# Weights converted with ScalarE's scaled high word and three VectorE operations, and new orders up to step 23

## The chip, the cores and the metric

The kernel runs on one core of a Trainium2 chip. The metric is the device time of one execution in microseconds (us), the median of several runs. The core has five engines that run side by side: TensorE (PE; matmuls, and PEld, its weight loads), VectorE (DVE), ScalarE (ACT), GpSimd (POOL) and SyncE (SP), which here issues the DMAs.

## The reference

A linear attention without a softmax, then two feed-forward layers, on 8 x 576 = 4608 tokens with 512 features. The weights come as float64 and q, k, v as float32.

```python
kv = np.einsum('bhsd,bhse->bhde', k, v)          # 8 x 8 heads, 576 tokens, 64 wide
out = np.einsum('bhsd,bhde->bhse', q, kv)
rms = np.sqrt(np.mean(out * out, axis=-1, keepdims=True) + 1e-06)
x = out / rms * g_norm                            # -> 4608 x 512

h = x @ w_in                                      # 512 x 2048
P = a[0] + a[1] * h + a[2] * h2 + a[3] * h3       # h2 = h*h, h3 = h2*h
Q = 1.0 + np.abs(b[0]) * np.abs(h) + np.abs(b[1]) * h2
x = (P / (Q + 1e-06)) @ w_out                     # 2048 x 512

h = (x @ w1) * (x @ w2) @ w3                      # 512 x 1024, 1024 x 1024
x = h @ w_out2                                    # 1024 x 512
```

## The kernel before

**Numbers.** Each matmul operand is split in a high and a low part (`hi`, `lo`, both in TensorE's reduced fp32 type), and a product is three matmuls. ScalarE casts the high part (L84), VectorE subtracts it for the low one (L85).

**Conversion of weights.** The chip gets a float64 weight as two 32-bit words, `hw` (sign, exponent and upper mantissa bits) and `lw`. `to_f32` (L144 to L165) builds the float32 from them; it is a generator that stops (`yield`) between its operations, so that a caller can put other work between them. `conv` runs it into a tile `ct` and queues the split of the weight, which is issued when two later conversions have gone ahead (`DEPTH`). There are 88 conversions: 32 of the first layer's `w_in` (`wa0` to `wa15`) and `w_out` (`wb0` to `wb15`), 32 of half the size for `w1` and `w2` in the background (`bg_conv`), and 24 for `w3` and `w_out2` (`cv_conv`).

**The start.** A string of letters (L458) sets the order in which work is issued until the first layer begins: `K` loads a tile of 128 tokens of k and v, `Q` one of q, `W` a weight, `C` converts one; `k` multiplies a tile into the batch's state (`kv`, copied into `kvbd`), `t` transposes q, `o` multiplies it with the state and squares the result, `r` and `n` make the norm and transpose it back, `x` writes the operand `xh`, `xl` of the first layer. A batch has 576 tokens, so its state needs four and a half tiles. All loads stand in SyncE's queue; k, v and q have two buffers each. Each engine works in the order in which its instructions were issued, and waits at the first whose inputs aren't there. Eleven of the 32 weights are converted here.

**The steps.** The first layer then runs in 192 steps `g` (12 blocks of 384 tokens by 16 slices of the 2048 columns). In step `g` TensorE does `l1(g)` (12 matmuls into `h`) and, three steps late, `l2(g - 3)` (12 matmuls into `acc`, which take `hi` and `lo`). Between them stands the function P/Q: `ew1(g)` on ScalarE (`a`, `z`, `n`), GpSimd (`s`, L543) and VectorE (L546, L548), `ewy(g)` on ScalarE, `ew2(g - 1)` on VectorE (L562, L564, L566) and `ew3(g - 2)`, which casts `hi` (L529) and subtracts `lo` (L531). The remaining 21 weights are converted in steps 0 to 22: a digit of `CONV` says how many in each step. The string `MIX[0]` says in which order the pieces of the generators are issued in these steps (`n` ew1, `l` ew3, `y` ewy, `s` ew2, `t` and `u` conversions); from step 23 on it is `MIX[1]`. Attention of later tiles is spread over the steps by a table (`at_step`).

After the first layer the second one runs in products of 256 columns (`c_slot`), then `w3` is multiplied with `w_out2`, and `d_slot` makes the output.

Of the kernel before, what the change touches and what calls it, by code (L numbers as in the profile page):

```python
# [12 lines left out]
AF = mybir.ActivationFunctionType  # L13
ALU = mybir.AluOpType
# [4 lines left out]
def linear_attention_two_moe_kernel(  # L19
# [24 lines left out]
    nc = tc.nc  # L44
# [35 lines left out]
    def f32(ap):  # L80
        return ap.bitcast(F32)
# [55 lines left out]
    def mix(order, **gens):  # L137

        for c in order:
            next(gens[c], None)  # L140
        for gen in gens.values():
            run(gen)

    def to_f32(raw, t, n=W):  # L144


        hw, lw = raw[:, :, 1], raw[:, :, 0]
        ti = t.bitcast(I32)
        nc.scalar.activation(out=ti, in_=f32(hw), func=AF.Copy, scale=0.47 * 2.0**15)
        nc.scalar.activation(out=t, in_=ti, func=AF.Sign)  # L150
        yield
        nc.vector.tensor_scalar(  # L152
            out=lw, in0=lw.bitcast(U32), scalar1=2.0**-29, scalar2=7.0, op0=ALU.mult, op1=ALU.min
        )
        yield
        nc.vector.scalar_tensor_tensor(
            out=lw, in0=hw, scalar=3, in1=lw, op0=ALU.logical_shift_left, op1=ALU.bitwise_or
        )
        yield
        nc.vector.tensor_scalar(  # L160
            out=lw, in0=lw, scalar1=0x7FFFFFFF, scalar2=0x40000000,
            op0=ALU.bitwise_and, op1=ALU.bitwise_xor,
        )
        yield
        nc.vector.tensor_tensor(out=t, in0=f32(lw), in1=t, op=ALU.mult)  # L165

    def f32_tile(n=W):
        return stp.tile([P, n], F32, tag="st", name="ct")
# [11 lines left out]
    def conv_flush():  # L180
        while pend:
            conv_on(0)

    def conv(raw, *stages):

        t = f32_tile(W)
        yield from to_f32(raw, t)
        pend.append((t, list(stages)))
        conv_on()
# [221 lines left out]
    with tc.manual_schedule():  # L411
# [23 lines left out]
        def w_next():  # L435
            kind, i = w_seq[n_cv[0]]
            n_cv[0] += 1
            return (conv_a if kind == "a" else conv_b)(i)
# [16 lines left out]
            "r": (n_rms, n_rsq), "n": (n_out, x_pe), "x": (x_out,),  # L455
        }
        whole = {"W": w_load, "C": w_conv, "F": conv_flush, "c": consts, "d": const_ops}
        for op in "KWCcKQkWKCWQWkCWtKQtkCKWFkdCkCoWWCQtoKoCrrnWCkWtKonKWrWWrCnxkKQWnQxxCxWW":  # L458
            if op in whole:
                whole[op]()  # L460
            else:
                i = count.get(op, 0)
                count[op] = i + 1
                for f in tile_ops[op]:
                    f(i)
# [93 lines left out]
        def ew2(g):  # L559
            e = st_[g]  # L560
            s, n, y = e["s"], e["n"], e["y"]
            nc.vector.scalar_tensor_tensor(out=s, in0=s, scalar=EPS_Q, in1=y, op0=ALU.add, op1=ALU.mult)  # L562
            yield
            nc.vector.scalar_tensor_tensor(out=n, in0=n, scalar=na[:, 0:1], in1=y, op0=ALU.add, op1=ALU.mult)  # L564
            yield
            nc.vector.scalar_tensor_tensor(out=n, in0=s, scalar=2.0, in1=n, op0=ALU.subtract, op1=ALU.mult)  # L566
# [12 lines left out]
        def do(g, place):  # L579
            for f, i in todo.get((g, place), ()):  # L580
                f(i)
# [17 lines left out]
        for i in range(T0, NTILE):  # L599
            j, t = divmod(i, TPB)  # L600
# [28 lines left out]
        def bg_conv(n):  # L629
            w = f32_tile(HW)  # L630
            yield from to_f32(bg_raw.pop(n), w, HW)
            nc.sync.dma_start(out=bg[n][2], in_=w)
# [221 lines left out]
        def cv_conv(n):  # L854
            w = f32_tile()
            run(to_f32(cv_raw.pop(n), w))
            nc.sync.dma_start(out=cv[n][1], in_=w)
# [185 lines left out]
                nc.scalar.copy(f["u"], f["b"])  # L1043
            e_load(n + 3)

        MIX = "nltutssnuyltntusutu", "nltysstnnltts"
        CONV = "11201102220020012111010"
        NG = NBA * MF
        LB = NG - MF
        prep = {}  # L1050
# [56 lines left out]
        for g in range(NG + SK):  # L1107
# [12 lines left out]
            if 0 <= g - 1 < NG:  # L1120
                gens["s"] = ew2(g - 1)
            if g < len(CONV):
                for x in "tuv"[:int(CONV[g])]:
                    gens[x] = w_next()
# [3 lines left out]
            if g - 2 in BG_AT:  # L1128
                gens["t"] = bg_conv(BG_AT.index(g - 2))
            mix("".join(x for x in MIX[g >= len(CONV)] if x in gens), **gens)  # L1130
            do(g, 2)
            do(g, 3)
            if g == len(CONV) - 1:
                conv_flush()
# [59 lines left out]
```

## Time and profile before

| | us |
|---|---|
| median of 3 runs | 1635.74 (1635.54 to 1637.78) |
| profiled execution, its own time | 1637.61 |
| its span | 1635.80 |
| TensorE busy (matmul) | 1550.0 (95%) |
| VectorE busy | 1337.7 (82%) |
| ScalarE busy | 1102.8 (67%) |
| GpSimd busy | 239.1 (15%) |

The span runs from the first to the last instruction of the profiled execution. Busy time is an average over stages with different limits: an engine that is busy for 82% of the span can be full in one stage and idle in the next. So the stages have to be looked at apart, and in each the question is which engine the others wait for. The granted clock is that of TensorE, as a share of full speed.

### The profile page before, as it was taken

The page shows a single profiled execution, that of the slowest core. Times are in us where ns is not written, and L with a number is a line of the kernel's source. Part 1 is how long each engine was busy: PE and PEld are TensorE (multiplying, and loading weights), DVE is VectorE, ACT ScalarE, POOL GpSimd, SP SyncE. Part 2 cuts the span into 40 slices and gives each one's busy share as a digit, 9 for nine tenths or more (in the row PEclk, how much of TensorE's full clock was granted, in tenths as well). Part 3 has the DMA queues.
Part 4 walks back from the last instruction along what each step waited for, and adds up shares of the span by engine and source line. Part 5 has one row for each costly group of instructions (what it writes and reads, how often), then busy time and mean ns, then how long its engine had stood idle before and what let it go on. Part 6 is the DMA issues. An engine that isn't in the chain of part 4 may idle for free.

```text
span 1635.8 us, 25683 instructions
## 1 busy us (share of the span) xinstructions
PE 1550.0 (95%) x9320; PEld 1506.2 (92%) x9320; DVE 1337.7 (82%) x2467; ACT 1102.8 (67%) x2197; POOL 239.1 (15%) x201
## 2 busy tenths in 40 slices
PE   4688899999999999999999998899999999999999
PEld 4687899999999999999999997899999998789999
DVE  5898987888989989999999889787677675578885
ACT  4787886787888888888878787554444443455554
POOL 0023322222222222222222221000000000000000
PEclk9798999999999999999999999999999999999999
DMA  9754234432111111111111011424534534334442
GB/s 243 188 148 126 58 79 103 104 81 59 52 30 52 32 51 43 52 49 39 40 42 54 6 46 36 139 91 152 186 104 158 169 112 139 117 125 155 156 158 88
DMA packets 202079, 157.92 MB, mean 97 GB/s; under 512 B 122848, under 2 KB 179936, under 8 KB 201952
## 3 DMA queue, kind: packets, MB, share of 16 engines
q1 hardware_dynamic: 201952, 156.28, 32.2%
q8 instruction: 73, 1.20, 0.3%
q14 instruction: 54, 0.44, 0.1%
HBM read 106.43 MB, written 49.81 MB: 96 GB/s over the span
## 4 chain that ended last, share of the span: by engine, by line
PE 67%; DVE 15%; ACT 3%; issue 2%; DMA 1%; POOL 0%; SPq 0%; DVEq 0%; ACTq 0%; POOLq 0%
PE acc L783 10%; PE h L90 6%; PE h L88 6%; PE h L89 6%; PE acc L496 5%; PE acc L991 5%; PE acc L493 5%; PE acc L494 5%; PE h L783 4%; PE kv L783 3%; PE at L783 3%; DVE n L564 3%; PE h L991 2%; DVE s L562 2%; PE kv L991 2%
## 5 line engine op out<-in xcount | busy, mean ns | idle before, releaser
L543 POOL TENSOR_TENSOR s<-z,a 128x384 f32<-128x384 f32 x192 | 237.5, 1237 | 774.5 <-ACT z L540 400.4
L564 DVE SCALAR_TENSOR_TENSOR n<-n,na,y 128x384 f32<-128x384 f32 x192 | 182.8, 952 | 0.0
L555 ACT ACTIVATE y<-s,epsq 128x384 f32<-128x384 f32 x192 | 118.2, 615 | 70.4 <-POOL s L543 70.2
L546 DVE TENSOR_TENSOR n<-n,h 128x384 f32<-128x384 f32 x192 | 104.8, 546 | 54.2 <-ACT n L541 54.1
L540 ACT ACTIVATE z<-a,ab 128x384 f32<-128x384 f32 x192 | 136.6, 711 | 6.4
L562 DVE SCALAR_TENSOR_TENSOR s<-s,y 128x384 f32<-128x384 f32 x192 | 134.3, 700 | 0.4
L539 ACT ACTIVATE a<-h 128x384 f32<-128x384 f32 x192 | 93.3, 486 | 54.3 <-PE h L90 52.0
L541 ACT ACTIVATE n<-h,na 128x384 f32<-128x384 f32 x192 | 126.2, 657 | 3.6 <-DVE lo L531 3.6
L548 DVE SCALAR_TENSOR_TENSOR n<-n,na,h 128x384 f32<-128x384 f32 x192 | 117.8, 614 | 6.0
L531 DVE TENSOR_TENSOR lo<-n,hi 128x384 fp32r<-128x384 f32 x192 | 106.2, 553 | 0.0
L566 DVE SCALAR_TENSOR_TENSOR n<-s,n 128x384 f32<-128x384 f32 x192 | 106.1, 553 | 0.0
L556 ACT ACTIVATE y<-y 128x384 f32<-128x384 f32 x192 | 101.2, 527 | 6.1
L529 ACT CAST hi<-n 128x384 fp32r<-128x384 f32 x192 | 96.6, 503 | 5.9 <-DVE n L566 5.8
L271 PE MATMUL kv<-vt,kt 128*128 128x128 f32 (+1 forms) x320 | 51.1, 310 | 14.8 <-DMA vt<-in_v_dram 13.9
L271 PEld LDWEIGHTS kv<-vt,kt 128*128 128x128 f32 (+1 forms) x320 | 47.7, 221 | 17.6 <-issue 12.2
L150 ACT ACTIVATE ct<-ct 128x512 f32<-128x512 int32 (+1 forms) x88 | 49.0, 556 | 2.8
L354 PE MATMUL at<-kvbd,qT 128*128 128x128 f32 (+1 forms) x216 | 28.7, 283 | 5.6 <-ACT qT L346 5.0
L354 PEld LDWEIGHTS at<-kvbd,qT 128*128 128x128 f32 (+1 forms) x216 | 26.3, 182 | 7.8 <-ACT qT L346 6.4
L825 ACT COPY p<-kv 128x384 f32<-128x384 f32 x24 | 11.5, 479 | 32.2 <-PE kv L783 20.7
L379 ACT ACTIVATE ny<-ms,epsn 128x8 f32<-128x8 f32 x36 | 11.1, 309 | 31.5 <-DVE ms L373 31.3
L840 ACT COPY u<-acc 128x384 f32<-128x384 f32 x24 | 11.5, 480 | 29.6 <-PE acc L783 29.5
L152 DVE TENSOR_SCALAR wb12r<-wb12r 128x512 int32<-128x512 uint32 x25 | 10.7, 427 | 24.8 <-DMA wb12r<-in_moe_w_dram 23.2
(1443 smaller groups left out, 5013.8 us busy)
## 6 DMA issues: line engine op xcount, KB each, us to landing
ed<-eo SPq DMA_DIRECT2D x48, 384.0 KB, 2.7
er<-ed SPq DMA_DIRECT2D x36, 512.0 KB, 3.8
x2d<-xev SPq DMA_DIRECT2D x48, 192.0 KB, 2.0
xr<-x2d SPq DMA_DIRECT2D x48, 192.0 KB, 4.0
out_dram<-o SPq DMA_DIRECT2D x36, 256.0 KB, 2.0
kt<-in_k_dram SPq DMA_DIRECT2D x32, 256.0 KB, 3.4
vt<-in_v_dram SPq DMA_DIRECT2D x32, 256.0 KB, 4.1
qt<-in_q_dram SPq DMA_DIRECT2D x32, 256.0 KB, 3.4
```

What stands on the lines that cost most here:

```text
L531: nc.vector.tensor_tensor(out=e["lo"], in0=e["n"], in1=f32(e["hi"]), op=ALU.subtract)
L540: nc.scalar.activation(out=z, in_=a, func=AF.Identity, scale=ab[:, 1:2], bias=ab[:, 0:1])
L541: nc.scalar.activation(out=n, in_=h, func=AF.Identity, scale=na[:, 3:4], bias=na[:, 2:3])
L543: nc.gpsimd.tensor_tensor(out=s, in0=z, in1=a, op=ALU.mult)
L546: nc.vector.tensor_tensor(out=n, in0=n, in1=h, op=ALU.mult)
L548: nc.vector.scalar_tensor_tensor(out=n, in0=n, scalar=na[:, 1:2], in1=h, op0=ALU.add, op1=ALU.mult)
L555: nc.scalar.activation(out=y, in_=e["s"], func=AF.Abs_reciprocal_sqrt, bias=epsq[:, 0:1])
L562: nc.vector.scalar_tensor_tensor(out=s, in0=s, scalar=EPS_Q, in1=y, op0=ALU.add, op1=ALU.mult)
L564: nc.vector.scalar_tensor_tensor(out=n, in0=n, scalar=na[:, 0:1], in1=y, op0=ALU.add, op1=ALU.mult)
L566: nc.vector.scalar_tensor_tensor(out=n, in0=s, scalar=2.0, in1=n, op0=ALU.subtract, op1=ALU.mult)
L783: nc.tensor.matmul(bank, lhsT=lh[:, sl], rhs=x, start=first and kk == 0 and n == 0, stop=kk == 1 and n == 2, skip_group_check=True,)
L991: nc.tensor.matmul(bank, lhsT=l[:, c, :], rhs=r, start=first and c == 0 and x == 0, stop=c == KH - 1 and x == 2, skip_group_check=True,)
```

## The change

`to_f32` no longer makes the sign apart. ScalarE copies the high word, read as a float32, with a scale of 2^-112 into `t`, which puts the exponent right but for three bits that are missing at the end; a second VectorE operation shifts it by 3 and joins the low word's bits, and a last one sets the sign bit from `t`. So ScalarE has one operation in place of two, and VectorE three in place of four; the second VectorE operation now reads what ScalarE wrote. The string of the start, `MIX[0]` and `CONV` get other orders of the same letters and digits that add up to the same 21.

```diff
         hw, lw = raw[:, :, 1], raw[:, :, 0]
         ti = t.bitcast(I32)
-        nc.scalar.activation(out=ti, in_=f32(hw), func=AF.Copy, scale=0.47 * 2.0**15)
-        nc.scalar.activation(out=t, in_=ti, func=AF.Sign)
+        nc.scalar.activation(out=t, in_=f32(hw), func=AF.Copy, scale=2.0**-112)
         yield
         nc.vector.tensor_scalar(
             out=lw, in0=lw.bitcast(U32), scalar1=2.0**-29, scalar2=7.0, op0=ALU.mult, op1=ALU.min
         )
         yield
         nc.vector.scalar_tensor_tensor(
-            out=lw, in0=hw, scalar=3, in1=lw, op0=ALU.logical_shift_left, op1=ALU.bitwise_or
+            out=lw, in0=ti, scalar=3, in1=lw, op0=ALU.logical_shift_left, op1=ALU.bitwise_or
         )
         yield
-        nc.vector.tensor_scalar(
-            out=lw, in0=lw, scalar1=0x7FFFFFFF, scalar2=0x40000000,
-            op0=ALU.bitwise_and, op1=ALU.bitwise_xor,
+        nc.vector.scalar_tensor_tensor(
+            out=ti, in0=ti, scalar=-0x80000000, in1=lw, op0=ALU.bitwise_and, op1=ALU.bitwise_or
         )
-        yield
-        nc.vector.tensor_tensor(out=t, in0=f32(lw), in1=t, op=ALU.mult)
...
-        for op in "KWCcKQkWKCWQWkCWtKQtkCKWFkdCkCoWWCQtoKoCrrnWCkWtKonKWrWWrCnxkKQWnQxxCxWW":
+        for op in "QKWQWKCWKWcCkCKKCQdtkWkktFktWCWooQoWWrCCWtWCoKWKrWnrkrKnCnQKkCxnxxWQCxWW":
...
-        MIX = "nltutssnuyltntusutu", "nltysstnnltts"
-        CONV = "11201102220020012111010"
+        MIX = "usnttulnslyutsntutu", "nltysstnnltts"
+        CONV = "21102011020121111110011"
```

The line numbers of the kernel after are four lower from there on (L562 is L558, L531 is L527, and so on); the conversion's VectorE operations are L151, L155 and L159.

In VectorE's queue, the larger part of a step with two conversions. Before, from the second conversion's first operation on:

```order
L152 TENSOR_SCALAR wb9r<-wb9r 128x512
L531 TENSOR_TENSOR lo<-n,hi 128x384
L156 SCALAR_TENSOR_TENSOR wa12r<-wa12r 128x512
L548 SCALAR_TENSOR_TENSOR n<-n,na,h 128x384
L160 TENSOR_SCALAR wa12r<-wa12r 128x512
L156 SCALAR_TENSOR_TENSOR wb9r<-wb9r 128x512
L566 SCALAR_TENSOR_TENSOR n<-s,n 128x384
L160 TENSOR_SCALAR wb9r<-wb9r 128x512
L165 TENSOR_TENSOR ct<-wa12r,ct 128x512
L85 TENSOR_TENSOR wa11hl<-ct,wa11hl 128x512
L165 TENSOR_TENSOR ct<-wb9r,ct 128x512
L85 TENSOR_TENSOR wb8hl<-ct,wb8hl 128x512
```

and now, from the same place of such a step on:

```order
L151 TENSOR_SCALAR wb8r<-wb8r 128x512
L542 TENSOR_TENSOR n<-n,h 128x384
L560 SCALAR_TENSOR_TENSOR n<-n,na,y 128x384
L527 TENSOR_TENSOR lo<-n,hi 128x384
L155 SCALAR_TENSOR_TENSOR wb8r<-ct,wb8r 128x512
L155 SCALAR_TENSOR_TENSOR wa11r<-ct,wa11r 128x512
L562 SCALAR_TENSOR_TENSOR n<-s,n 128x384
L544 SCALAR_TENSOR_TENSOR n<-n,na,h 128x384
L159 SCALAR_TENSOR_TENSOR ct<-ct,wa11r 128x512
L85 TENSOR_TENSOR wa9hl<-ct,wa9hl 128x512
L159 SCALAR_TENSOR_TENSOR ct<-ct,wb8r 128x512
L85 TENSOR_TENSOR wa10hl<-ct,wa10hl 128x512
```

The third operation of each conversion is gone, the second reads `ct`, both second ones stand behind `lo`, and the product L560 (L564 before) stands right behind the one that reads `h`.

In ScalarE's queue in the start, around the load of the norm's function table. Before:

```order
L149 ACTIVATE ct<-wb1r 128x512
L150 ACTIVATE ct<-ct 128x512
L84 CAST wb0hl<-ct 128x512
L346 COPY qT<-acc_269 128x512
L367 ACTIVATE sq<-h 128x512
L367 ACTIVATE sq<-at 128x512
L149 ACTIVATE ct<-wa5r 128x512
L150 ACTIVATE ct<-ct 128x512
L84 CAST wa4hl<-ct 128x512
L379 ACT_TABLE_LOAD
L379 ACTIVATE ny<-ms,epsn 128x8
```

and now:

```order
L342 COPY qT<-acc_222 128x512
L149 ACTIVATE ct<-wb0r 128x512
L363 ACTIVATE sq<-h 128x512 x2
L363 ACTIVATE sq<-at 128x512
L375 ACT_TABLE_LOAD
L375 ACTIVATE ny<-ms,epsn 128x8
L377 ACTIVATE ny_269<-ny 128x8
L149 ACTIVATE ct<-wa4r 128x512
L149 ACTIVATE ct<-wb1r 128x512
L84 CAST wb0hl<-ct 128x512
```

The squares, the table load and the first norm now stand ahead of the words of wa4 and wb1, which stood ahead of them before.

In SyncE's queue, the loads up to the fifth tile of k and v (the one that comes in two halves). Before:

```order
L104 DMA wa1r<-in_moe_w_in_dram 128x4x256
L246 DMA kt<-in_k_dram 128x8x64
L246 DMA vt<-in_v_dram 128x8x64
L104 DMA wa2r<-in_moe_w_in_dram 128x4x256
L246 DMA qt<-in_q_dram 128x8x64
L104 DMA wa3r<-in_moe_w_in_dram 128x4x256
L104 DMA wb0r<-in_moe_w_out_dram 128x1024
L246 DMA kt<-in_k_dram 128x8x64
L246 DMA vt<-in_v_dram 128x8x64
L246 DMA qt<-in_q_dram 128x8x64
L246 DMA kt<-in_k_dram 64x8x64 x2
L246 DMA vt<-in_v_dram 64x8x64 x2
```

and now:

```order
L104 DMA wa2r<-in_moe_w_in_dram 128x4x256
L242 DMA kt<-in_k_dram 128x8x64
L242 DMA vt<-in_v_dram 128x8x64
L104 DMA wa3r<-in_moe_w_in_dram 128x4x256
L205 DMA co_a<-in_moe_a_dram 128x4
L206 DMA co_b<-in_moe_b_dram 128x2
L208 DMA gcol<-in_g_norm_dram 64x1 x2
L242 DMA kt<-in_k_dram 128x8x64
L242 DMA vt<-in_v_dram 128x8x64
L242 DMA kt<-in_k_dram 64x8x64 x2
L242 DMA vt<-in_v_dram 64x8x64 x2
```

One weight (wb0) and one tile of q went behind the fifth tile; the small constants came here from the queue's front.

## Rows read from the trace of the kernel before

**Rows 1.** Stretches: length, busy time (instructions) of each engine, clock, DMA share, GB/s.
```profile
core 0: us, PE busy (x) PEld busy (x) DVE busy (x) ACT busy (x) POOL busy (x), PEclk, DMA share, GB/s
0.00:60.80 60.80, 29.13 (x128) 26.27 (x129) 35.97 (x72) 29.18 (x54) 1.67 (x9) 0.86 0.80 199
60.80:206.10 145.30, 122.72 (x674) 116.14 (x673) 137.05 (x253) 115.81 (x217) 44.94 (x23) 0.92 0.50 133
206.10:955.00 748.90, 741.27 (x4414) 723.11 (x4413) 671.27 (x1231) 609.31 (x1200) 177.88 (x157) 1.00 0.20 53
955.00:1635.80 680.80, 656.83 (x4110) 640.71 (x4108) 493.37 (x913) 348.47 (x729) 14.63 (x13) 0.99 0.39 127
```

**Rows 2.** TensorE in order of time: start, duration, instruction; the first `l1` matmul.
```profile
60.82 0.58 PE L88 MATMUL h<-xh,wa0hl 128*128 128x384 f32 x1
```

**Rows 3.** What TensorE waited for, 60.8 to 206.1 us: total, times, longest.
```profile
PE acc L496 <- DVE lo L531: 9.4, 5, 2.9
PE acc L493 <- ACT xev L518: 4.7, 1, 4.7
```

**Rows 4.** ScalarE's two passes: duration in ns (least/median/most), first and last start.
```profile
L149 ACT ACTIVATE ct<-wb12r x25: 667/686/703, 174.8 to 1357.2; 128x512 int32<-128x512 f32 x25
L150 ACT ACTIVATE ct<-ct x88: 418/632/638, 7.9 to 1357.9; 128x512 f32<-128x512 int32 x56, 128x256 f32<-128x256 int32 x32
```

**Rows 5.** VectorE in order of time in a step with two conversions.
```profile
126.46 0.42 DVE L152 TENSOR_SCALAR wa12r<-wa12r 128x512 int32<-128x512 uint32 x1
...
130.94 0.42 DVE L160 TENSOR_SCALAR wa12r<-wa12r 128x512 int32<-128x512 int32 x1
131.28 0.69 DVE L156 SCALAR_TENSOR_TENSOR wb9r<-wb9r 128x512 int32<-128x512 int32 x1
...
135.09 0.55 DVE L562 SCALAR_TENSOR_TENSOR s<-s,y 128x384 f32<-128x384 f32 x1
```

**Rows 6.** What VectorE waited for, 60.8 to 206.1 us (all that there is).
```profile
DVE n L546 <- ACT n L541: 5.0, 4, 1.9
DVE kve L295 <- ACT kve L294: 1.3, 1, 1.3
DVE ny L387 <- ACT ny L381: 1.2, 2, 0.6
```

**Rows 7.** Two products: groups from 60.8 to 206.1 us (busy, mean ns); L564's range.
```profile
L564 DVE SCALAR_TENSOR_TENSOR n<-n,na,y 128x384 f32<-128x384 f32 x22 | 24.0, 1090 | 0.0
L562 DVE SCALAR_TENSOR_TENSOR s<-s,y 128x384 f32<-128x384 f32 x22 | 14.0, 636 | 0.0
...
L564 DVE SCALAR_TENSOR_TENSOR n<-n,na,y x192: 602/615/1445, 69.4 to 1019.9; 128x384 f32<-128x384 f32 x192
```

**Rows 8.** DMA issues: count, size of one, median us to landing (q, v as k).
```profile
kt<-in_k_dram SPq DMA_DIRECT2D x32, 256.0 KB, 3.4
...
wa0r<-in_moe_w_in_dram SPq DMA_DIRECT2D x1, 512.0 KB, 5.3
```

**Rows 9.** In order of time, the start: the state's copy, table load, last `xl`.
```profile
31.18 0.43 DVE L290 COPY kvbd<-kv 64x256 f32<-64x256 f32 x1 [3.40 <-ACT kvbd L289]
...
42.16 1.28 ACT L379 ACT_TABLE_LOAD   x1
...
59.02 1.40 DVE L406 SCALAR_TENSOR_TENSOR xl<-acc,gneg,xh 128x512 fp32r<-128x512 f32 x2
```

**Rows 10.** VectorE in order of time: one conversion alone, its first, third and last operation.
```profile
31.64 0.43 DVE L152 TENSOR_SCALAR wa4r<-wa4r 128x512 int32<-128x512 uint32 x1
...
32.84 0.43 DVE L160 TENSOR_SCALAR wa4r<-wa4r 128x512 int32<-128x512 int32 x1
33.37 0.69 DVE L165 TENSOR_TENSOR ct<-wa4r,ct 128x512 f32<-128x512 f32 x1
```

**Rows 11.** What VectorE waited for, 27 to 61 us.
```profile
DVE ct L165 <- ACT ct L150: 3.6, 3, 2.0
...
DVE ms L373 <- ACT sq L367: 2.6, 1, 2.6
```

**Rows 12.** What TensorE waited for, 255 to 955 us.
```profile
PE acc L496 <- DVE lo L531: 4.7, 11, 0.6
```

## The prediction

> **What bounds the kernel now.** I read the stretches first: busy time and granted clock of each engine in four pieces of the span [rows 1]. The span falls into a start of 60.8 us that ends with the first `l1` matmul, the 23 steps that still convert weights (60.82 us, [rows 2], to the first matmul of step 23 at 206.1), and the rest. From 206 us on TensorE is busy for 741.3 of 748.9 and 656.8 of 680.8 us: it is the bound there, and VectorE or ScalarE work saved in it is worth only what TensorE waits for. In the 23 converting steps it is the other way round. VectorE is busy for 137.05 of 145.30 us; TensorE is busy for 122.7, much of it at the half clock (mean 0.92), and its waits there are for VectorE's `lo` (9.4 us) and for ScalarE's eviction of `acc` behind it (4.7 us) [rows 3]. In the start neither is full (VectorE 36.0, TensorE 29.1 of 60.8); a chain of loads, attention products, norms and conversions ends last. So the change is worth what VectorE loses in the 23 steps, plus what the new order does to the start.
>
> **The conversion itself.** Before, one conversion of 128x512 is two ScalarE and four VectorE operations; now one and three. There are 88: 11 in the start, 21 in the 23 steps (the digits of both tables add up to 21), 32 half-sized ones later, 24 in the last stretch.
> - ScalarE's Sign pass goes (0.632 us). The new scaled pass reads the same strided word as the old one (median 0.686 us, [rows 4]); only the type that it writes differs. I take it as equal. ScalarE is busy for 115.8 of 145.3 us, so the 21 x 0.63 = 13.3 us count for nothing by themselves.
> - VectorE's third operation, a tensor_scalar, goes. It lasts 0.42 us, but in a full queue the next operation starts earlier: 130.94 to 131.28, so 0.34 us each [rows 5]. The two that stay have the same size and the same count of inputs as the old second operation (0.69 us, [rows 5]). The new last one reads one contiguous and one strided tensor as a scalar_tensor_tensor, which no row shows; nearest are this 0.69 us with both strided, and 0.55 us for 384 contiguous columns (0.73 us if scaled to 512, too high since part of it is fixed). I take no change; bounds -0.05 to +0.1 us each.
> In the 23 steps: 21 x 0.34 = **7.1 us less** on the engine that bounds them (bounds of the price: 5 to 8.2).
>
> **The new step order.** `MIX` puts the previous step's first product ahead, the high half later, and both conversions' long operations behind `lo`; `CONV` replaces six steps with two conversions and eight with none by four and six. VectorE's idle time in the stretch is 145.30 - 137.05 = 8.25 us, 5.0 of it waits for ScalarE's `n` [rows 6], that is for `h` of a TensorE that was late after a run of twos: a two-conversion step costs 126.46 to 135.09 = 8.63 us on VectorE [rows 5], against 145.3 / 23 = 6.3 us for the mean step. Flatter counts let the queue absorb the steps without conversion. I take half of the idle time, **4 us less** (bounds 0 to 8). What is late next is still VectorE: 137 - 7 = 130 us of work in about 134.
> The new wait: the second VectorE operation now needs ScalarE's word, one operation earlier than the sign was needed. Behind a waiting one stand `lo` and the step's last products, and for `lo` TensorE waits. In the order that word is issued ahead of the high half and of `y`, with three or more VectorE operations between; before, ScalarE ran several operations ahead of VectorE in these steps. I cost it at nothing; without that cover it is at most one ScalarE pass, 0.69 us, times 21.
>
> **GpSimd's product.** The second product of the previous step (L564) lasts 1.09 us in the mean here, 24.0 us over 22, and L562 0.636 [rows 7]; over the whole span L564 lasts between 0.60 and 1.45 us [rows 7], the long ones beside GpSimd's multiply. Against 0.61 and 0.55 (an L562 alone, [rows 5]) the stretch loses 22 x 0.48 + 22 x 0.09 = 12.5 us so. The new order has L564's successor right behind the product that reads `h`, in every step. If every step pays 0.75 us it is 16.5, +4 us; if the third operation's absence lets GpSimd through earlier, it falls. I take **+1 us** (bounds -4 to +4).
> The Trainium skill (SBUF — State Buffer, "Who interferes with whom") says that a VectorE instruction with two SBUF inputs, or in a 2-port mode, contends with a GpSimd one that reads SBUF, and one blocks the other whole. The 1.45 us against 0.60 agree, and by that rule the removed operation, a 2-port one, also unblocks GpSimd while the re-ordered product meets it more often. By the rule the sum stays within the bounds of the rows.
>
> **The start.** Up to the last piece of the fifth K/V tile, which closes the first batch's state, the queue moved five K/V pairs, five weights and three Q: 5 x 512 + 5 x 512 + 3 x 256 = 5888 KB; now five, four and two, 5120 KB [rows 8]. At 199 GB/s [rows 1] 768 KB are 3.9 us. The buffers of K and V are two, so the fifth waits for the third's products, which gives some of it back; I take 3.5: VectorE's copy of the state moves from 31.18 to 27.7 us [rows 9]. From it to the end of the third `xl` (59.02 + 1.40 = 60.42) are 29.2 us, in which VectorE does five conversions of 2.42 us (dependent ones: 31.64 to 33.37 + 0.69). The third operation is 0.53 of it (32.84 to 33.37, [rows 10]), so one costs 1.89 now. New, from the copy to the third `xl`: six conversions, since wb0's moved behind the copy, 6 x 1.89 = 11.3, with the other 29.2 - 12.1 = 17.1, and a wait that the order adds: ScalarE now does all three squares and its 1.28 us table load [rows 9] before the words of wa4 and wb1, and VectorE's second operation on wa4 stands in front of everything else there. I estimate the last square to end at 36 us (three products after the state, then the square); with 1.28 for the table, some 0.6 for the first norm and 0.69 for the pass, wa4's word comes at about 38.7, and VectorE is there at 34.8: 3.9 us, and about as much at wb0, behind the third copy of `qT`, where the old order waits 3.6 us for the Sign pass and 2.6 for the fourth square [rows 11]; net some +2.4. 27.7 + 11.3 + 17.1 + 2.4 = 58.5: **2.3 us earlier** than 60.8. Bounds: 8 earlier if the waits are hidden, 2 later if the fifth tile comes no sooner.
>
> **After step 23.** TensorE waits 4.7 us, 11 times, for `lo` between 255 and 955 us [rows 12]; 32 half conversions give each up to 0.2 us. I take **1 us less** (0 to 4.7). The last 24 lie beside a full TensorE: nothing.
>
> **Sum:** -7.1 - 4 + 1 - 2.3 - 1 = -13.4 us. The profiled execution took 1637.61 us (span 1635.80 and 1.81 around it), so 1624.2 of its kind; the median of the runs is 1635.74, 1.87 under it, so 1622.3. I forecast **1622 us**, own range 1613 to 1629.
>
> **Rivals.**
> 1. Only the removed work counts: the flatter `CONV` gains nothing, every step pays GpSimd's stall (+4), and the start's new waits eat its loads: -7.1 + 4 - 1 = -4 us, 1632. For it: VectorE's 95% leave little idle time. Against: the 5.0 us of waits for `n` sit around the runs of two.
> 2. Larger: TensorE's full waits vanish and with them the half clock, and the start hides its waits: -7.1 - 8 - 4 (GpSimd's bound) - 8 = -27, 1609. For it: the clock of 0.92 in the stretch and 0.86 in the start [rows 1]. Against: VectorE's 130 us of work remain above TensorE's.
> 3. Slower: the added wait decides. If ScalarE, which has the step's three passes, `y` behind GpSimd and the high half in its queue, delivers the word a pass late, VectorE stands 0.69 us at its second operation in each of 21 conversions and, in order, everything behind it; 14.5 us, with the stall's 4 us: +18.5 - 7.1 - 2.3 = +9, 1645. It decides from (7.1 + 2.3 - 4) / 21 = 0.26 us a conversion on. For it: at the start VectorE does wait for the Sign pass [rows 11], and the word is now needed earlier. Against: in the 23 steps VectorE's waits for ScalarE are for `n`, `kve` and `ny`, none for a conversion [rows 6].
> 4. No change within 0.2%: the order's ends all fall on the bad side, +2 at the start, +4 beside GpSimd and nothing from `CONV`, and eat the removed operation: 2 + 4 - 7.1 = -1 us, 1635. For it: three new orders at once, none of which a row shows. Against: VectorE's full stretch, where less work must show unless something new takes its place.
>
> **Chances.** Forecast with its own range 0.62; smaller gain (rival 1) 0.16; larger (2) 0.08; no change 0.07; slower 0.07. A difference under 0.2% (3.3 us) can't be told from none here. Rival 1 lies partly inside that: faster 0.85, same 0.08, slower 0.07. Range for 8 in 10: 1608 to 1633, from the larger case to rival 1.
>
> **What would show it.** The 23 steps last some 134 us instead of 145.3, and VectorE's busy time in them falls to about 130; the conversion's three operations last 0.43, 0.69 and 0.69 us; the first `l1` matmul starts at 58 to 59 us, with VectorE waiting for ScalarE's words of wb0 and wa4 before it; L564's successor has a mean of 1.1 us or more in the stretch; from step 23 on the time is the same to 2 us. I am wrong if VectorE's waits for `ct` appear in the steps, if the new last operation lasts over 0.8 us, or if the stretch keeps its length with VectorE less busy, which would make TensorE or ScalarE its bound.

## The result and the profile after

The kernel after takes 1615.66 us (median of 4 runs, 1614.03 to 1617.62); before, with one more run, 1636.20. The ratio is 0.9874, 95% interval [0.9856, 0.9891]. The forecast was 1622, the range 1608 to 1633: faster, as said, by 20.5 us where 13.4 were expected. The profiled execution has a span of 1613.0 us (1614.78 with what lies around it), 22.8 less than before. Cut at the same places of the program as [rows 1] (first `l1`, step 23, and 933.4 for 955):

```profile
core 0: us, PE busy (x) PEld busy (x) DVE busy (x) ACT busy (x) POOL busy (x), PEclk, DMA share, GB/s
0.00:56.50 56.50, 28.02 (x129) 25.21 (x129) 30.74 (x60) 22.78 (x43) 1.66 (x9) 0.68 0.89 221
56.50:186.80 130.30, 117.20 (x674) 109.58 (x673) 126.00 (x231) 103.70 (x194) 29.26 (x23) 0.97 0.55 145
186.80:933.40 746.60, 739.57 (x4414) 723.65 (x4413) 663.89 (x1202) 598.88 (x1170) 181.19 (x157) 1.00 0.20 54
933.40:1613.00 679.60, 656.36 (x4110) 641.57 (x4108) 483.13 (x889) 332.83 (x705) 14.45 (x13) 0.98 0.38 127
```

The start is 4.3 us shorter, the 23 converting steps 15.0, the two long pieces 2.3 and 1.2. In the converting steps VectorE is still the fullest engine: its busy time fell by 11.05 us and its idle time from 8.25 to 4.30. GpSimd's busy time fell from 44.9 to 29.3 although its 23 multiplies are the same.

What TensorE and then VectorE waited for in the converting steps (total, times, longest):

```profile
PE at L350 <- ACT qT L342: 5.6, 2, 4.2
PE acc L492 <- DVE lo L527: 2.7, 7, 0.7
PE h L88 <- DVE n L544: 2.2, 4, 0.6
```

```profile
DVE n L542 <- ACT n L537: 2.3, 2, 2.0
DVE ny L383 <- ACT ny L377: 1.2, 2, 0.6
```

The waits for `lo` (9.4 us) and behind them for the eviction (4.7) of [rows 3] are down to 2.7 and none, VectorE's waits for `n` from 5.0 [rows 6] to 2.3, and no wait of VectorE for `ct` is there. The two products of [rows 7] in the same stretch (busy, mean ns), and the conversion's operations over the whole span, by the group of the last full-sized ones, 25 of 56 (ns: least, median, most):

```profile
L558 DVE SCALAR_TENSOR_TENSOR s<-s,y 128x384 f32<-128x384 f32 x22 | 14.4, 655 | 0.1
L560 DVE SCALAR_TENSOR_TENSOR n<-n,na,y 128x384 f32<-128x384 f32 x22 | 14.4, 654 | 0.0
```

```profile
L149 ACT ACTIVATE ct<-wb12r x25: 661/675/701, 159.1 to 1332.5; 128x512 f32<-128x512 f32 x25
L151 DVE TENSOR_SCALAR wb12r<-wb12r x25: 417/427/431, 162.3 to 1332.2; 128x512 int32<-128x512 uint32 x25
L155 DVE SCALAR_TENSOR_TENSOR wb12r<-ct,wb12r x25: 680/694/698, 164.1 to 1333.2; 128x512 int32<-128x512 int32 x25
L159 DVE SCALAR_TENSOR_TENSOR ct<-ct,wb12r x25: 691/693/1245, 165.7 to 1334.0; 128x512 int32<-128x512 int32 x25
```

The product's mean fell from 1090 to 654 ns. The long cases sit mostly elsewhere now: in the converting steps 9 of the 21 new last operations (L159) take 1.24 to 1.26 us for 0.69 alone. VectorE's waits in the start, 25 to 57 us, in place of [rows 11]:

```profile
DVE wa2hl L85 <- ACT wa2hl L84: 4.3, 1, 4.3
DVE wa4r L155 <- ACT ct L149: 3.7, 1, 3.7
DVE wb0r L155 <- ACT ct L149: 3.2, 1, 3.2
```

### The profile page after: what moved, and what is told of

Read it like the earlier page. It is cut to its first block, busy times and chain, and to the rows that moved or that the text cites. A ratio compares the mean times of both kernels' runs of the same rounds, so it can differ in the third digit from the quotient of the medians.

```text
span 1613.0 us, 25500 instructions
## 1 busy us (share of the span) xinstructions
PE 1541.2 (96%) x9320; PEld 1500.0 (93%) x9320; DVE 1303.8 (81%) x2379; ACT 1058.2 (66%) x2109; POOL 226.6 (14%) x201
## 4 chain that ended last, share of the span: by engine, by line
PE 72%; DVE 18%; ACT 4%; issue 3%; SPq 1%; POOL 1%; DMA 1%; DVEq 0%; ACTq 0%; POOLq 0%
PE acc L779 11%; PE h L90 6%; PE h L88 6%; PE h L89 6%; PE acc L492 6%; PE acc L987 5%; PE acc L489 5%; PE acc L490 5%; PE h L779 5%; PE kv L779 3%; PE at L779 3%; DVE n L560 3%; PE h L987 2%; DVE n L562 2%; PE kv L987 2%
## 5 line engine op out<-in xcount | busy, mean ns | idle before, releaser
L539 POOL TENSOR_TENSOR s<-z,a 128x384 f32<-128x384 f32 x192 | 224.9, 1171 | 765.5 <-ACT z L536 423.9
L560 DVE SCALAR_TENSOR_TENSOR n<-n,na,y 128x384 f32<-128x384 f32 x192 | 178.9, 932 | 0.0
L542 DVE TENSOR_TENSOR n<-n,h 128x384 f32<-128x384 f32 x192 | 104.7, 545 | 55.7 <-ACT n L537 55.2
L558 DVE SCALAR_TENSOR_TENSOR s<-s,y 128x384 f32<-128x384 f32 x192 | 127.4, 664 | 1.1
L527 DVE TENSOR_TENSOR lo<-n,hi 128x384 fp32r<-128x384 f32 x192 | 105.7, 551 | 0.0
L562 DVE SCALAR_TENSOR_TENSOR n<-s,n 128x384 f32<-128x384 f32 x192 | 105.7, 550 | 0.0
L821 ACT COPY p<-kv 128x384 f32<-128x384 f32 x24 | 11.5, 479 | 42.4 <-PE kv L779 31.1
L821 ACT COPY p<-acc 128x384 f32<-128x384 f32 x24 | 11.5, 480 | 38.1 <-PE acc L779 30.8
L836 ACT COPY u<-acc 128x384 f32<-128x384 f32 x24 | 11.5, 479 | 33.6 <-PE acc L779 33.6
L796 DVE TENSOR_TENSOR acc<-acc,u 128x384 f32<-128x384 f32 x24 | 13.6, 566 | 19.2 <-ACT u L836 18.8
```

What stands on the lines that cost most here:

```text
L527: nc.vector.tensor_tensor(out=e["lo"], in0=e["n"], in1=f32(e["hi"]), op=ALU.subtract)
L539: nc.gpsimd.tensor_tensor(out=s, in0=z, in1=a, op=ALU.mult)
L542: nc.vector.tensor_tensor(out=n, in0=n, in1=h, op=ALU.mult)
```

## The experiments

All are timed against the kernel before on the same chip, so two of them are compared by how far each lies under the kernel before beside it; after lies 20.5 us under. "Before" and "after" are the two kernels. "Stretch" is the time from the first `l1` matmul to that of step 23, "late steps" from step 32 to the last `l1` (steps 32 to 191). In before they last 145.3 and 753.5 us, in after 130.3 and 751.0. A profile is one execution: in those of the four kernels that share after's start the first `l1` comes at 55.6 to 58.0 us, and in those of the six that share its late steps these last 749.8 to 751.0, so smaller differences there say little.

### The parts of the change apart

**The conversion alone**, in the old orders:

```diff
-        for op in "QKWQWKCWKWcCkCKKCQdtkWkktFktWCWooQoWWrCCWtWCoKWKrWnrkrKnCnQKkCxnxxWQCxWW":
+        for op in "KWCcKQkWKCWQWkCWtKQtkCKWFkdCkCoWWCQtoKoCrrnWCkWtKonKWrWWrCnxkKQWnQxxCxWW":
...
-        MIX = "usnttulnslyutsntutu", "nltysstnnltts"
-        CONV = "21102011020121111110011"
+        MIX = "nltutssnuyltntusutu", "nltysstnnltts"
+        CONV = "11201102220020012111010"
```

> Kernel before with the new conversion alone, all three orders old. Theory A (VectorE's work bounds the 23 steps, each of the three parts adds its own): steps 0 to 22 lose 7 us, the start about 3 (five dependent conversions by 0.53 us), the later steps 3: about 13 us under before, 1623; L564's mean in the stretch stays near 1.1 us. Rival B (the orders made the gain, the removed operation is filled with waits): 1 to 4 us under before, the stretch within 3 us of 145. Rival C (the removed 2-port operation is what frees GpSimd): L564's mean falls to 0.8 or less and the gain is 16 us or more.

Measured: 1622.07 us, ratio 0.9918 [0.9904, 0.9932]. First `l1` 2.2 us earlier than before, stretch 138.5 (6.8 less), late steps 750.0 (3.5 less). It lies 13.2 us under before, as theory A had it. L560's mean in the stretch is 1019 ns, so the removed operation by itself doesn't take the product away from GpSimd's multiply, and rival C fails.

**The orders alone**, with the old `to_f32` in the new start, `MIX` and `CONV`:

> Kernel before with the three new orders and the old conversion. Theory A: CONV's flatter counts give 4 us, MIX's fewer stalls 4, the start 2: about 10 us under before, 1626, and VectorE's busy time in the 23 steps 131 to 134 us. Rival B (orders made the gain): 16 us or more under before. Rival C (the freed port comes from the removed operation): 6 us or less, and the second product keeps a mean over 0.95 us.

Measured: 1632.35 us, 0.998 [0.997, 0.999]. The stretch is 139.4 us (5.9 less), but the nine steps behind it take 52.7 us for 48.9 (VectorE is busy for 41.6 of them; what holds them up stays open), and the late steps 752.4. So the orders give 2.9 us by themselves (before was 1635.27 beside it) and 7.3 on top of the conversion (20.5 - 13.2). L564's mean is 649 ns: the orders do take the product away from the multiply. But here the stall falls on the conversion's third operation (L160), of which 9 of 21 take over 0.8 us for 0.42 alone, and VectorE's busy time falls by 2.2 us, less than theory A had. The two stretches, the conversion's first:

```profile
58.64:197.17 138.53, 120.49 (x674) 113.65 (x673) 130.13 (x231) 103.28 (x195) 31.70 (x23) 0.94 0.52 139
```

```profile
58.16:197.60 139.44, 119.73 (x676) 111.14 (x675) 134.85 (x250) 115.53 (x215) 29.91 (x23) 0.96 0.51 135
```

Alone, the conversion leaves VectorE idle for 8.4 us, as before; the orders take the idle time down to 4.6, but with the old conversion's 134.9 us of work.

**After with the old `MIX[0]`:**

```diff
-        MIX = "usnttulnslyutsntutu", "nltysstnnltts"
+        MIX = "nltutssnuyltntusutu", "nltysstnnltts"
```

> Kernel after with the old MIX in steps 0 to 22. Theory A (MIX moved the product beside GpSimd's multiply): the second product's mean in the stretch back to 1.0 us or more, GpSimd's multiply back to 1.8 us, the stretch 4 us longer, 1619 to 1620. Rival (the removed operation freed GpSimd, MIX does nothing): mean 0.7, time within 1 us of after. Rival (MIX costs through the later high half): 1 to 3 us under after.

Measured: 1622.32 us, 0.9923 [0.9908, 0.9938], 13.0 under before, so 7.6 us of after's gain are gone; stretch 136.9, 6.5 of it beyond after's, VectorE busy for 130.0. A step with one conversion, VectorE in order of time, with the old `MIX` first (start, duration):

```profile
155.00 0.42 DVE L151 TENSOR_SCALAR wb11r<-wb11r 128x512 int32<-128x512 uint32 x1
...
155.80 1.36 DVE L560 SCALAR_TENSOR_TENSOR n<-n,na,y 128x384 f32<-128x384 f32 x1
...
159.15 0.68 DVE L159 SCALAR_TENSOR_TENSOR ct<-ct,wb11r 128x512 int32<-128x512 int32 x1
...
160.82 0.42 DVE L151 TENSOR_SCALAR wa15r<-wa15r 128x512 int32<-128x512 uint32 x1
```

```profile
151.00 0.41 DVE L151 TENSOR_SCALAR wb11r<-wb11r 128x512 int32<-128x512 uint32 x1
...
151.80 0.60 DVE L560 SCALAR_TENSOR_TENSOR n<-n,na,y 128x384 f32<-128x384 f32 x1
...
154.40 1.25 DVE L159 SCALAR_TENSOR_TENSOR ct<-ct,wb11r 128x512 int32<-128x512 int32 x1
...
156.64 0.42 DVE L151 TENSOR_SCALAR wa15r<-wa15r 128x512 int32<-128x512 uint32 x1
```

In this step the multiply of GpSimd meets the product in the old order (0.76 us more) and the conversion's last operation in the new one (0.57 more); the step takes 5.82 us in the one and 5.64 in the other. Here the new order doesn't avoid the stall, it puts it on an operation that loses less by it. Over the stretch the long cases (over 0.8 us) of L560 go from 10 with the old `MIX` to 3, and its mean from 967 to 654 ns; those of the last operation go from none to 9, those of L558 from 5 to 3. VectorE's busy time is 4.0 us less by the new `MIX`, and its idle time 2.6 less. The multiply's own mean, 1344 ns with the old `MIX`, stays far from the expected 1.8 us.

**After with the old `CONV`:**

```diff
-        CONV = "21102011020121111110011"
+        CONV = "11201102220020012111010"
```

> Kernel after with the old CONV. Theory A (the runs of twos made TensorE late and then VectorE wait for it): the eviction wait of some 4 us and VectorE's waits for n of 5 us come back in steps 8 to 12, 4 us over after, 1620. Rival (the counts per step don't matter, only VectorE's total does): within 1 us of after. Rival (the parts only work together): 6 us or more over after.

Measured: 1617.85 us (1616.07 to 1622.21), 0.9901 [0.9886, 0.9917]. In the profiled execution VectorE waits 10.0 us for `n` in the stretch (after: 2.3), which lasts 136.5 us, and TensorE's wait for the eviction is back with 2.9; but that execution is the slowest of the five. By the medians, each beside its before, `CONV` is worth 3.6 us, and the interval overlaps after's. That the idle time comes back is shown by the trace; the size stays open.

**After with the old start:**

```diff
-        for op in "QKWQWKCWKWcCkCKKCQdtkWkktFktWCWooQoWWrCCWtWCoKWKrWnrkrKnCnQKkCxnxxWQCxWW":
+        for op in "KWCcKQkWKCWQWkCWtKQtkCKWFkdCkCoWWCQtoKoCrrnWCkWtKonKWrWWrCnxkKQWnQxxCxWW":
```

> Kernel after with the old string of the start. Theory A: the first l1 matmul at 58 us instead of 56.5 (the new conversion shortens the old start too, by some 3 us), so 1 to 2 us over after. Rival (the new string made the 4.3 us of the start): l1 at 60.5, 4 us over after.

Measured: 1615.73 us, 0.9879 [0.9864, 0.9894]: the string's change is worth nothing that can be told from noise (19.5 us under before, after 20.5). The first `l1` is 2.3 us later, step 8 only 0.2. Start and steps 0 to 7, of this kernel and then of after:

```profile
0.00:58.80 58.80, 28.32 (x128) 25.81 (x129) 31.64 (x61) 22.79 (x43) 1.66 (x9) 0.77 0.81 206
58.80:104.25 45.45, 38.97 (x240) 37.35 (x238) 42.59 (x81) 35.91 (x70) 11.59 (x8) 0.96 0.77 197
```

```profile
0.00:56.50 56.50, 28.02 (x129) 25.21 (x129) 30.74 (x60) 22.78 (x43) 1.66 (x9) 0.68 0.89 221
56.50:104.02 47.52, 40.57 (x239) 38.95 (x237) 43.40 (x82) 35.95 (x70) 11.62 (x8) 0.92 0.69 180
```

Up to step 8 VectorE has 74.2 and 74.1 us of work and is idle for 30.0 and 29.9: the new string moved its waits from the squares and other words to the words of wb0 and wa4, and behind a first `l1` that comes earlier steps 0 to 7 take 2.1 us longer.

### What the stalls beside GpSimd cost

GpSimd's multiply became a memset of the same tile, which only writes, in before and in after; the first layer's denominator is left out by it:

```diff
-            nc.gpsimd.tensor_tensor(out=s, in0=z, in1=a, op=ALU.mult)
+            nc.gpsimd.memset(s, 1.0)
```

> Kernel before with GpSimd's multiply replaced by a memset of the same tile, so that GpSimd reads nothing; the denominator of the first layer is left out by it. Theory A (GpSimd's reads hold VectorE up): L564's mean in the stretch falls to 0.62 us and VectorE's busy time by 10 to 13; the stretch by 8 to 12 us. Rival (the long L564s come from their scalar operand or from waiting for y): the mean stays over 0.9 us.

> Kernel after with GpSimd's multiply replaced by a memset of the same tile; the denominator of the first layer is left out by it. Theory A (the new order's gain is that fewer stalls beside GpSimd are left): VectorE's busy time in the stretch falls by 4 to 8 us from 126, less than in the kernel before. Rival (stalls only changed place, onto the conversions' last operation): it falls by 10 to 13, as much as before.

Measured: 1599.85 us, 0.9788 [0.9773, 0.9802], and 1588.35, 0.9719 [0.9706, 0.9732]. The stretch and the late steps, of before with the memset and then of after with it:

```profile
60.24:190.87 130.63, 116.89 (x675) 110.12 (x674) 125.51 (x255) 116.07 (x220) 11.60 (x23) 0.96 0.55 147
238.69:973.44 734.75, 731.34 (x4379) 726.42 (x4378) 597.81 (x1240) 603.60 (x1202) 66.51 (x159) 1.00 0.19 52
```

```profile
55.58:176.78 121.20, 114.92 (x674) 110.98 (x673) 116.78 (x231) 101.25 (x195) 9.88 (x23) 0.96 0.57 153
225.91:962.15 736.24, 732.81 (x4379) 728.00 (x4378) 593.16 (x1211) 591.89 (x1171) 66.67 (x159) 1.00 0.19 53
```

The stretch gets 14.7 us shorter in before and 9.1 in after, so up to 5.6 of the 15.0 us are stalls that became cheaper: up to, since the memset is also shorter than the multiply and `s` can come earlier by it. VectorE's busy time in the stretch, in which the stalls themselves lie, falls by 11.5 us in before and by 9.2 in after, 2.3 apart; the 9.2 lie between what theory A (4 to 8) and its rival (10 to 13) had for after, so most of the stalls only changed place. The Trainium skill (SBUF — State Buffer, "Who interferes with whom") says that a VectorE instruction with two SBUF inputs contends with a GpSimd one that reads and not with one that only writes; the L560 group agrees, with a mean of 609 ns beside the memset. The late steps are 15 to 19 us shorter beside the memset, though TensorE is busy for 98.6% of them in after: its 741 us of "busy" are 8 us more than beside the memset for the same 4379 matmuls.

### An operation put back, and one more taken away

**After with a third VectorE operation**, a mask that leaves the values as they are, ahead of the last one in all 88 conversions:

```diff
+        nc.vector.tensor_scalar(
+            out=lw, in0=lw, scalar1=0x7FFFFFFF, scalar2=0x7FFFFFFF,
+            op0=ALU.bitwise_and, op1=ALU.bitwise_and,
+        )
```

> Kernel after with a third VectorE operation put back into every conversion, a tensor_scalar of the same shape as the removed one that changes nothing. Theory A (the removed operation is worth its place in VectorE's queue): 21 x 0.34 = 7 us in the stretch, 2 to 4 in the start and 4 to 5 in the later steps: 12 to 15 us over after, 1628 to 1631. Rival (the gain of the conversion comes from the Sign pass that ScalarE is spared): 3 us or less over after.

Measured: 1639.75 us, 1.0033 [1.002, 1.0046], 5.0 over before, so 25.5 over after, more than was expected; the rival (the gain comes from ScalarE's Sign pass) fails. By the trace (25.0 over after): start 2.7, stretch 11.0 (0.52 for each operation of 0.34), steps 23 to 31 1.0, late steps 8.8, the rest 1.5. The stretch was expected to lose about its 7, all that follows 4 to 5. In the stretch the operation takes the stall upon itself, as in the orders alone: 11 of 21 last over 0.8 us. In the late steps 32 operations of 0.30 us cost 0.28 each, nearly all of their length. But that is not the price of the operation that the change removed: before and the orders alone have it too, at a place of its own (here it has no `yield` and stands straight ahead of the last one), and their late steps last 753.5 and 752.4 us, 1.4 to 3.7 over those of the kernels without it, some 0.1 us for each. So what it costs there depends on where it stands; why, no run here shows.

**After with the low word on ScalarE**, so that VectorE has two operations and ScalarE two passes (the scale is a little low so that rounding can't reach 8; a weight's last three bits can differ):

```diff
-        nc.vector.tensor_scalar(
-            out=lw, in0=lw.bitcast(U32), scalar1=2.0**-29, scalar2=7.0, op0=ALU.mult, op1=ALU.min
-        )
+        nc.scalar.activation(out=lw, in_=lw.bitcast(U32), func=AF.Copy, scale=0.936 * 2.0**-29)
```

> The kernel after with the conversion's first VectorE operation (the low word, 0.43 us) made by ScalarE instead, so that VectorE has two operations a conversion and ScalarE two passes; all orders as after. Theory 1, VectorE's queue is what the converting steps, and the background conversions later, go by: the third operation put back cost +24 us (11 in the 23 steps, 10 later), so one operation less of the same size gives back about as much or somewhat less: VectorE busy 126.0 - 21 x 0.34 = 119 us in the stretch, the stretch 130.3 -> 121 to 124, l1 no later, the part from step 32 on 2 to 5 us shorter, 1600 to 1607 us in all. Theory 2, ScalarE has no room left for it: 103.7 + 21 x 0.69 = 118 us of its own in the stretch, its low word comes late behind n, y and the high half, VectorE's second operation waits for it (waits on L151 of ScalarE appear), and the stretch stays at 129 to 134 us: 1613 to 1622.

Measured: 1610.26 us (1606.78 to 1615.72), 0.986 [0.9836, 0.9885]. Its stretch and late steps, and VectorE's waits in the stretch:

```profile
55.21:188.01 132.80, 119.88 (x675) 112.35 (x674) 117.42 (x209) 112.82 (x215) 32.40 (x23) 0.94 0.54 143
237.64:981.14 743.50, 736.80 (x4380) 725.37 (x4378) 660.07 (x1178) 611.30 (x1203) 185.20 (x159) 1.00 0.19 52
```

```profile
DVE n L540 <- ACT n L535: 8.7, 6, 3.2
DVE lo L525 <- ACT hi L523: 3.4, 5, 1.0
```

VectorE has 8.6 us less to do and the stretch is 2.5 longer: VectorE waits now for ScalarE's `n` and `hi`, and once, 1.1 us, for the low word. The first theory fails there; the late steps are 7.5 us shorter, more than it had. The time lies between the two theories.

**After with the words first in the start:**

```diff
-        for op in "QKWQWKCWKWcCkCKKCQdtkWkktFktWCWooQoWWrCCWtWCoKWKrWnrkrKnCnQKkCxnxxWQCxWW":
+        for op in "QKWQWKCWKWcCkCKKCQdtkWkkFtkCtWWCooQoWCrWWtWCoKWKrWnrkrKnCnQKkCxnxxWQCxWW":
```

> The kernel after with six letters of the start's string moved: ScalarE has the words of wb0 and wa4 ahead of the third qT and the squares, and that of wb1 ahead of the norm's table load; the first sum of squares goes behind wb1's conversion on VectorE. Loads as after. Theory 1, VectorE's idle time in the start (4.3 + 3.7 + 3.2 us of waits for ScalarE between 25 and 38 us) is time of the bound, since its backlog in steps 0 to 8 has to be worked off: 3 to 6 us of these waits go and the kernel gains 2 to 4 us (1612 to 1614), the first l1 and step 8 both earlier by that. Theory 2, the start is bounded by attention's chain (qT, o, squares, norm, xt, xl), which this order delays by two ScalarE passes: the waits for the words go, but VectorE waits for squares and norms in their place, step 8 comes at the same time to 1 us, and the time is 1615 to 1617.

Measured: 1611.20 us (1609.07 to 1613.42), 0.9868 [0.9851, 0.9884]. By the trace the first `l1` comes at 52.4 and step 8 at 99.3 us, 4.1 and 4.7 earlier than in after, and the gain stays (span 5.7 shorter): VectorE's work up to step 8 is 74.0 us again, its idle time 25.3. The waits for the words of wb0 and wa4 are 0.3 and none. By ratios to before the interval overlaps after's (22.6 us under before, after 20.5), so the gain is shown by the trace's stretches and not by the times; the last run of this section, with the same start, has its first `l1` at 53.4 and step 8 at 100.2.

**Both edits:**

> Both edits together: the low word on ScalarE and the words first in the start. If both first theories hold, the gains add: 1597 to 1605. If ScalarE has become the bound of the start by the second pass (each word now two passes of 0.69 us ahead of qT and the squares), the start's gain is lost or turned round and the time is that of the low word alone or 1 to 3 us above it.

Measured: 1609.12 us, 0.9848 [0.9833, 0.9862]. The second pass on ScalarE eats the start's gain: first `l1` at 55.3 (55.2 with the low word alone), stretch 133.2, late steps 743.9.

**The words first, and the low word on ScalarE only in the 32 background conversions:**

```diff
-        nc.vector.tensor_scalar(
-            out=lw, in0=lw.bitcast(U32), scalar1=2.0**-29, scalar2=7.0, op0=ALU.mult, op1=ALU.min
-        )
+        if n == W:
+            nc.vector.tensor_scalar(
+                out=lw, in0=lw.bitcast(U32), scalar1=2.0**-29, scalar2=7.0, op0=ALU.mult, op1=ALU.min
+            )
+        else:
+            nc.scalar.activation(out=lw, in_=lw.bitcast(U32), func=AF.Copy, scale=0.936 * 2.0**-29)
```

> The kernel after with the start's words first (as in the run of that alone) and the low word on ScalarE only in the 32 half-sized conversions of the background, from step 34 on; the start and the 23 converting steps keep three VectorE operations. Theory 1, the low word on ScalarE loses in the start and the converting steps, where ScalarE's queue is full (the stretch became 2.5 us longer, with waits for hi and n), and wins behind them, where VectorE's lo comes late for TensorE (7.5 us less from step 32 to the last l1): here the first l1 and step 23 stay 4 to 5 us earlier than after, the stretch stays at 129 to 131 us, and from step 32 to the last l1 it is 743 to 745 us for 751; together 10 to 13 us less than after, 1602 to 1606 us. Theory 2, the 7.5 us came from another phase of the steps behind the longer stretch and not from where the word is made: then step 32 to the last l1 keeps 749 to 752 us and the time is that of the words first alone, 1609 to 1613.

Measured: 1604.01 us (1603.25 to 1607.27), 0.9812 [0.9796, 0.9829], 31.7 us under before and by the intervals under after. Stretch 129.7, late steps 743.4, as the first theory had it. What TensorE's weight loads waited for in the late steps, first in before, then in after, here, and with the third operation put back:

```profile
PEld acc L496 <- DVE lo L531: 17.3, 27, 3.7
```

```profile
PEld acc L492 <- DVE lo L527: 14.0, 22, 3.7
```

```profile
PEld acc L495 <- DVE lo L530: 7.5, 9, 3.7
```

```profile
PEld acc L496 <- DVE lo L531: 24.2, 36, 3.7
```

The late steps last 753.5, 751.0, 743.4 and 759.8 us: in this order too they follow the weight loads' waits for `lo`. Beside the memset these waits are 2.7 us in before and in after, and the late steps 734.8 and 736.2.

## Why the prediction was right, and where its sizes were off

**The removed operation** (-7.1 us): right. The conversion alone shortens the stretch by 6.8, VectorE's busy time there by 6.9. In the new orders it is worth more, 8.9 of busy time against the orders alone, because there the removed operation carries stalls. The scaled pass (675 ns for 686) and the two remaining operations (694 and 693 ns for 690) cost what was taken.

**Idle time** (-4): right in its mechanism; that it is half of the idle time was a choice without a row, and that it fell by just 3.95 us is luck. The waits for `n` that carried the argument went from 5.0 to 2.3, and are 10.0 with the old `CONV`, 4.8 with the old `MIX`.

**GpSimd's product** (+1): the step that failed, with the wrong sign; the value was at the bound of -4. The text let L564's successor meet the multiply in up to every step and pay 0.75 us, so that its mean would be 1.1 us or more; the mean is 654 ns. It is long in 3 of 22 cases, by 0.3 us; the conversion's last operation is in 9 of 21, by 0.57. VectorE's busy time fell by 11.05: some 7 for the operation and 4 for this, which is also what the old `MIX`, put back by itself, costs (130.0 for 126.0). The memset runs put the stalls themselves at 2.3 of it, so the rest of the 4 stays open. That the stretch's sum is then -7.1 - 4 - 4 = -15.1, with 15.0 measured, adds no proof, since busy and idle time make up the length.

**The start** (-2.3): the waits for the words were foreseen at 3.9 us each, and are 3.2 and 3.7; the state's copy [rows 9] at 27.7, and is at 26.9; the first `l1` came at 56.5, not 58.5. Of the wait that the order adds, the text's own parts, 3.9 + 3.9 - 3.6 - 2.6, give 1.6 and not 2.4. But above all the term ended at the wrong place. What counts is VectorE's idle time up to step 8, and in that the string gives nothing; of the 4.3 us only the conversion's stay, 2.2 by the first `l1` of the conversion alone. The gain that was to be had lies in waits that the new string left standing, as the words first show.

**After step 23** (-1): the mis-sized term; 3.5 us from step 23 on, and 4.7 from step 32. The step read TensorE's 99% of busy time as "the bound" and priced only the matmuls' waits [rows 12]. Its weight loads wait too, 17.3 us for `lo` in before's late steps and 14.0 in after's, and over the runs the length of these steps follows them. VectorE's work is not free there: the removed operation is worth 1.4 to 3.7 us in the late steps, another taken away 7.5, and one put back right ahead of the last costs 8.8.

**Rivals.** The added wait (slower) never came about: in the stretch VectorE waits for no word. It did in the start, where it was expected. "Only the removed work" was priced at 4 us; the conversion alone gives 13.2 (1622). The larger gain had the right GpSimd bound, twice the idle time and the wrong start. It counted on the clock: but a mean of 0.92 between full and half is some 16% of the stretch at the half clock, not "much" of TensorE's work, and after's mean is 0.97. The forecast's 1622 is the time of the conversion alone by accident: orders worth -3 beside the start were in it, and 7.3 were found.

## What to carry to other kernels

A stall between two engines is priced by the instruction that it falls on: look in the order at what stands beside the other engine's reads, and at what another operation in its place would lose. An engine's busy share near 100% doesn't make it the bound while its loads still wait for another engine; take one operation away, or put one back, and see what the time does. What is put back has to stand where it stood, or it measures another thing. A start counts up to where its backlog is worked off, not up to its first matmul.

## What the hardware showed beside it

The multiply on GpSimd lasted 1979 ns in the mean in before's stretch, 1293 in after's, and 1.00 us at its shortest: GpSimd is held up too, and less where VectorE meets it less. Half-sized operations of 0.30 us, beside a TensorE that is busy for 98%, cost 0.28 us each in one place of the order and some 0.1 in another. The same VectorE work in after's late steps took 12% less busy time when GpSimd read nothing (671 to 593 us).
